# First projections by token tile, loads in a new order, and transposes by DMA in a two-branch attention kernel

## The chip, the cores and the metric

The kernel runs on one core of one Trainium2 chip. The metric is the device time of one execution in microseconds (us), the median of the runs shown. Engines are named as in the profile: PE (TensorE, matmuls), PEld (its weight loads), DVE (VectorE), ACT (ScalarE), POOL (GpSimd), SP (SyncE, which issues most DMAs).

## The reference

```python
def _A_ref(x, wqkv, wo):                       # softmax attention, 32 heads of 16, S = 2048, D = 512
    q, k, v = ...                              # x @ wqkv, split by head
    scores = jnp.einsum("bhqd,bhkd->bhqk", q, k) * (Dh ** -0.5)
    o = jnp.einsum("bhqk,bhkd->bhqd", _softmax(scores), v)
    return o.reshape(B, S, D) @ wo
def _B_ref(x, wqkv, w_phi, wo):                # linear attention with a learned feature map
    pq, pk = einsum("bhsd,hdf->bhsf", q, w_phi), einsum("bhsd,hdf->bhsf", k, w_phi)
    phi = concatenate([softmax(p), softmax(-p)])        # for q and for k
    o = (phi_q @ (phi_k^T v)) / (phi_q @ sum(phi_k) + 1e-6)
    return o.reshape(B, S, D) @ wo
g = _sigmoid((x * gate_w).sum(-1, keepdims=True))
return g * _A_ref(...) + (1 - g) * _B_ref(...)
```

All inputs are bf16; x is 2048 x 512.

## The kernel before

Branch A (softmax attention) carries the time. Its scores are cut into 2048 tiles of 128 keys x 512 queries; four tiles that share keys and queries (four heads) make a pack, 512 packs in all, in the order of query chunk (4 of 512 rows), pair of heads, key tile. For most tiles PE makes the scores in PSUM (`_scores`, L925), ACT takes the exponential of three and then of two tiles in turn (`_exp`, L976), and PE multiplies by V (`_values`, L1045). The score tiles of ACT lie in a ring of five PSUM banks, so the scores of one exponential wait until the exponential before the last has read its banks. 210 tiles go to DVE instead: `SHARES` says how many in each group of 16 packs; `_vector_batch` gathers up to five, copies their scores out of PSUM as integers (`v_bits`, L826) into `vt`, and makes the exponential by a cubic (L848 to L852, L836). `vt` lies over `xn`, the x that was loaded, so its first writes wait until x has been read for the last time.

Branch B is spread between the packs: `_b_fuse` multiplies its q and k weights by the feature map, for which they are transposed (WT, L1146) and multiplied by the block-diagonal `wphi` (L1155); then come keys (`_b_keys`), values and queries, all exponentials on DVE.

At the start x must be transposed, as every projection contracts over its 512 columns. `_x_transpose` does this on PE (L622, four 128x128 blocks per tile of 128 tokens) and DVE or ACT copies them from PSUM to `xT` (L635). For the first 512 tokens, `_proj_q0` and `_proj_k0` project 256 tokens at a time (L682, L651), so that the first packs can start with half the queries; DVE masks q into two sides (L689) and copies k (L665). Weights of branch A lie in `WA` (for q, k and v: a first block of 128 columns, then 384), of branch B in `WB`.

The order of the work on each engine is not written by hand. Every operation is given to a `Plan` with an estimated cost, a latency, its dependences, a priority (`prio`, a due time in packs) and an earliest pack (`rel`); `Plan.order` simulates the engines and writes each engine's list, and the engines then run their lists strictly in order, waiting on semaphores. So a waiting instruction holds up everything behind it on its engine, SP's list of DMAs included. Constants of `_Kernel` (`LEAD`, `QDUE`, `K0`, `SHARES` and so on) steer the plan.

SP's list in the kernel before starts: x tiles 0-1, 2-3, 4-7, the V block of WA, x 8-11, x 12-15, WB for k, eight small DMAs of w_phi into the diagonal blocks of `wphi` (zeroed by POOL before, L542), three blocks of WA, WB for v, WB for q, four transposes into WT (wait for WB for k), four small DMAs of gate_w, eight DMAs that bring the next q into place (L708), WoA, WoB, four transposes into WT (for q). The Q and K blocks of WA are issued by ACT.

Of the kernel before, what the change touches and what calls it, by code (L numbers as in the profile page):

```python
# [10 lines left out]
P = 128  # L11
# [339 lines left out]
class _Kernel:  # L351
# [43 lines left out]
    def _memory(self, ctx):  # L395
# [29 lines left out]
        self.WB = sb("WB", [P, 4, 3 * D], BF16)  # L425
        self.WoA = sb("WoA", [P, 4, D], BF16)
        self.WoB = sb("WoB", [P, 4, D], BF16)
        self.wphi = sb("wphi", [P, 4, P], BF16)
        self.kT = sb("kT", [P, 4, S], BF16)
# [11 lines left out]
        self.WT = sb("WT", [P, 4, D], BF16)  # L441
# [8 lines left out]
        self.onTB = self.WT  # L450
        self.outt = self.WB[:, 0:2, 2 * D:3 * D]
# [21 lines left out]
    def _loads(self):  # L473
# [5 lines left out]
        self.b_WoA, self.b_WoB, self.b_wphi, self.b_gw = B(), B(), B(), B()  # L479
        WA3 = self.A_wqkv.rearrange("(c p) j -> p c j", p=P)  # L480
        x4 = self.x2d.rearrange("(t p) d -> p t d", p=P)

        def load_x(j, halves, lat):
            for h in halves:
                t0, t1 = (4 * j + 2 * h, 4 * j + 2 * h + 2) if len(halves) == 1 else (4 * j, 4 * j + 4)
                if h and len(halves) == 2:
                    continue
                self.dma("SP", f"x{j}{h}", lambda e, t0=t0, t1=t1: e.dma_start(self.xn[:, t0:t1, :], x4[:, t0:t1, :]),
                         writes=[self.b_xn[j][i] for i in halves], prio=-50 + j, lat=lat, cost=0.53)

        def load_wa(s, part, eng, prio, lat):
            lo, hi = (0, P) if part == 0 else (P, D)
            self.dma(eng, f"wa{s}{part}", lambda e: e.dma_start(  # L493
                self.WA[:, s, :, lo:hi], WA3[:, :, D * s + lo:D * s + hi]), writes=[self.b_WA[s][part]], prio=prio,
                lat=lat, cost=0.54 if part == 0 else 1.5)

        load_x(0, [0], 2.8)
        load_x(0, [1], 3.6)
        load_wa(1, 0, "ACT", -50, 3.1)
        load_wa(0, 0, "ACT", -49.9, 3.5)  # L500
        load_x(1, [0, 1], 5.0)
        load_wa(2, 0, "SP", -48.5, 5.4)
        load_x(2, [0, 1], 6.2)
        load_x(3, [0, 1], 7.2)
        load_wa(1, 1, "SP", -46, 7.0)
        load_wa(0, 1, "SP", -45, 6.5)
        load_wa(2, 1, "SP", -44, 6.0)
# [964 lines left out]
```

## Time and profile before

| | |
|---|---|
| runs | 847.53, 847.71, 847.96 us; median 847.71 |
| the profiled execution | 847.48 us, of which the span of the core's work is 845.7 |
| busy in the span | ACT 834.1 us, PE 814.9, DVE 814.6, POOL 7.6 |
| first exponential starts; last one ends | 8.12 us; 840.4 us |
| granted TensorE clock | full (1.00) |

How to read the profile: its chain follows the work that ended last back to the start, with the share of the span of each engine and line. A group's line gives engine, operation, out<-in with shapes and count, then busy time, mean ns of one, and the idle time of the engine just before with what ended it. A timeline line gives start and length in us; instructions of one kind in a row are merged (x12); the bracket is the idle time before. Lines with a "q" behind the engine (SPq) are the issue of DMAs, not their transfer. For DMAs the profile gives the time from issue to landing. In tables by stretch of time, the columns are the stretch, its length, the busy time of each engine, the granted clock, the mean busy share of the 16 DMA engines and GB/s.

### The profile page before, as it was taken

How to read it: one execution, taken by the hardware profiler on the slowest of the kernel's cores; microseconds unless marked ns; L12 is line 12 of the kernel's file. 1: busy time of each engine (PE TensorE's matmuls, PEld its weight loads, DVE VectorE, ACT ScalarE, POOL GpSimd, SP SyncE). 2: the span in 40 equal slices, each digit the busy share in tenths (PEclk: the TensorE clock that was granted, in tenths of full speed). 3: DMA queues.
4: the chain of work that ended last, by engine and by line, in shares of the span. 5: the costliest groups of instructions: out<-in, count | busy, mean ns of one | idle time of the engine just before them, and what ended most of it. 6: DMA issues, size and time to landing. Idle time of an engine off the chain costs nothing.

```text
span 845.7 us, 20062 instructions
## 1 busy us (share of the span) xinstructions
PE 814.9 (96%) x8992; PEld 268.1 (32%) x8992; DVE 814.6 (96%) x1037; ACT 834.1 (99%) x740; POOL 7.6 (1%) x14
## 2 busy tenths in 40 slices
PE   9999999999999999999999999999999999999997
PEld 5324333333322322232323223232322223322244
DVE  5889999999999999999999999999999999999994
ACT  7999999999999999999999999999999999999997
POOL 3000000000000000000000000000000000000000
PEclk9999999999999999999999999999999999999999
DMA  9300000000000000020201102010101102000000
GB/s 261 96 1 8 1 8 1 2 8 5 5 2 7 2 2 8 2 43 3 39 8 33 32 8 44 14 45 13 39 8 27 32 14 39 8 2 1 2 2 27
DMA packets 45222, 19.00 MB, mean 22 GB/s; under 512 B 34897, under 2 KB 45137, under 8 KB 45137
## 3 DMA queue, kind: packets, MB, share of 16 engines
q1 hardware_dynamic: 43936, 17.40, 8.8%
q8 instruction: 70, 1.15, 0.5%
q10 hardware_dynamic: 1200, 0.33, 0.2%
q14 instruction: 16, 0.12, 0.0%
HBM read 6.31 MB, written 2.10 MB: 10 GB/s over the span
## 4 chain that ended last, share of the span: by engine, by line
ACT 97%; SPq 1%; POOL 1%; DMA 0%; PE 0%; DVE 0%; issue 0%; POOLq 0%
ACT ET L976 97%; SPq L1146 1%; DMA WT<-WB 0%; SPq L546 0%; POOL V L535 0%; POOL qT L541 0%; SPq L493 0%; SPq L512 0%; POOL V L537 0%; POOL wphi L542 0%; PE ps L1045 0%; DVE xT L1420 0%; PE ps L1410 0%; PE ps L1155 0%; PE ps L925 0%
## 5 line engine op out<-in xcount | busy, mean ns | idle before, releaser
L976 ACT ACTIVATE ET<-ps 128x1536 bf16<-128x1536 f32 x735 | 831.6, 1389 | 2.1 <-PE ps L925 1.9
L925 PE MATMUL ps<-qT,kT 32*128 32x512 bf16 (+2 forms) x2248 | 317.1, 364 | 24.2 <-ACT ET L976 18.3
L1054 PE MATMUL ps<-kT,zero 128*32 128x512 bf16 (+1 forms) x3272 | 271.0, 384 | 0.0
L1045 PE MATMUL ps<-ET,V 128*32 128x512 bf16 (+2 forms) x2014 | 194.6, 364 | 0.3 <-ACT ET L976 0.3
L925 PEld LDWEIGHTS ps<-qT,kT 32*128 32x128 bf16 x2248 | 83.7, 91 | 311.0 <-ACT ET L976 225.9
L826 DVE TENSOR_SCALAR vt<-ps 128x512 uint32<-128x512 f32 x210 | 137.4, 680 | 2.6 <-PE ps L925 1.9
L836 DVE SCALAR_TENSOR_TENSOR vu<-vt,vu 128x2560 int16<-128x2560 uint32 (+4 forms) x44 | 118.5, 2693 | 0.4
L1054 PEld LDWEIGHTS ps<-kT,zero 128*32 128x32 bf16 x3272 | 72.8, 95 | 116.3 <-issue 89.7
L851 DVE TENSOR_TENSOR vf<-vf 128x2560 f16<-128x2560 f16 (+4 forms) x60 | 81.9, 1365 | 0.5
L848 DVE TENSOR_SCALAR vf<-vt 128x2560 f16<-128x2560 uint8 (+4 forms) x60 | 81.9, 1365 | 0.2
L1045 PE MATMUL ps<-vu,V 128*32 128x512 bf16 (+1 forms) x234 | 76.5, 360 | 0.0
L1045 PEld LDWEIGHTS ps<-ET,V 128*32 128x32 bf16 x2014 | 55.4, 96 | 51.5 <-issue 30.5
L852 DVE TENSOR_TENSOR vu<-vu,vf 128x2560 f16<-128x2560 f16 (+4 forms) x44 | 62.4, 1419 | 0.2
L651 PE MATMUL ps<-WB,xT 128*128 128x512 bf16 x192 | 55.6, 383 | 0.5 <-DVE T L1074 0.2
L1230 DVE TENSOR_TENSOR vt<-bq,bsum 128x2048 uint32<-128x2048 bf16 x16 | 36.5, 2282 | 0.2
L1234 DVE SCALAR_TENSOR_TENSOR bq<-vt,bq 128x2048 int16<-128x2048 uint32 x16 | 36.5, 2280 | 0.1
L651 PE MATMUL ps<-xT,WA 128*128 128x512 bf16 (+1 forms) x128 | 35.5, 376 | 0.0
L850 DVE TENSOR_SCALAR vu<-vf 128x2560 f16<-128x2560 f16 (+4 forms) x44 | 34.5, 785 | 0.3
L1074 DVE STREAM_TRANSPOSE T<-ps 128x512 f32<-128x512 f32 (+1 forms) x35 | 23.1, 659 | 3.5 <-PE ps L1045 3.5
L1045 PEld LDWEIGHTS ps<-vu,V 128*32 128x32 bf16 x234 | 20.9, 96 | 12.6 <-issue 8.5
L1187 DVE TENSOR_SCALAR bq<-ps 128x512 bf16<-128x512 f32 x32 | 21.5, 682 | 1.6 <-PE ps L651 1.6
L651 PEld LDWEIGHTS ps<-WB,xT 128*128 128x128 bf16 x192 | 14.3, 97 | 26.1 <-issue 13.5
(88 smaller groups left out, 407.6 us busy)
## 6 DMA issues: line engine op xcount, KB each, us to landing
qT<-qraw SPq DMA_DIRECT2D x120, 16.0 KB, 1.8
xn<-in_A_x_dram SPq DMA_DIRECT2D x3, 512.0 KB, 6.7
WB<-in_B_wqkv_dram SPq DMA_DIRECT2D x3, 512.0 KB, 8.3
out_dram<-WB SPq DMA_DIRECT2D x12, 128.0 KB, 1.7
WA<-in_A_wqkv_dram SPq DMA_DIRECT2D x3, 384.0 KB, 5.8
xn<-in_A_x_dram SPq DMA_DIRECT2D x2, 256.0 KB, 3.8
WoA<-in_A_wo_dram SPq DMA_DIRECT2D x1, 512.0 KB, 4.1
WoB<-in_B_wo_dram SPq DMA_DIRECT2D x1, 512.0 KB, 5.0
```

The costliest lines, as they stand in the source:

```text
L651: mm = op("PE", lambda e, c=c: e.matmul(self._bank(job)[:, 0:n], lhs(c), rhs(c), start=(c == 0), stop=(c == 3)), self.c_pe(n), reads=reads ...
L826: parts.append(op("DVE", lambda e, j=j, job=job: e.tensor_scalar(vt[:, j, :], self._bank(job), SCALE * LOG2E * 2.0 ** 24, 2.0 ** 31, op0=A ...
L836: o = op("DVE", lambda e: e.scalar_tensor_tensor(out=flat(vu).bitcast(I16), in0=flat(vt), scalar=2.0 ** -17, in1=flat(vu), op0=ALU.mult, o ...
L848: ("_frac", two, lambda e: e.tensor_scalar(vf, frac, 1 / 256, ROOT, op0=ALU.mult, op1=ALU.add), [b_vt], [b_vf]),
L851: ("_sq", two, lambda e: e.tensor_tensor(vf, vf, vf, ALU.mult), [b_vf], [b_vf]),
L852: ("_cube", two, lambda e: e.tensor_tensor(vu, vu, vf, ALU.mult), [b_vf, b_vu], [b_vu]),
L925: ins = e.matmul(out[u][:, cols], self.kT[32 * i:32 * i + 32, cp, kt * TOK:(kt + 1) * TOK], self.qT[32 * i:32 * i + 32, s, q], start=True, ...
L976: o = plan.op("ACT", lambda e: e.activation(self.ET[:, a % NS:a % NS + n, :], self.ps[:, a % NR:a % NR + n, :], ACT.Exp, scale=SCALE), sel ...
L1045: ins = e.matmul(self._bank(ot)[32 * i:32 * i + 32, to], self.V[:, kt, g8 // 2, v0:v0 + 32], tile[:, cols], start=first and j == 0, stop=o ...
L1054: ins = e.matmul(self._bank(ot)[32 * i:32 * i + 32, lo:QCH], self.zero[:], self.kT[:, 0, lo:QCH], start=False, stop=False, tile_position=( ...
L1230: op("DVE", lambda e: e.tensor_tensor(vt.rearrange("p (g f i) -> p g f i", f=DH, i=4), x, top, ALU.subtract), self.c_dve(n), reads=[b, sel ...
L1234: op("DVE", lambda e: e.scalar_tensor_tensor(out=flat.bitcast(I16), in0=vt, scalar=2.0 ** -17, in1=half, op0=ALU.mult, op1=ALU.add), self. ...
```

## The change

- The first two x tiles are projected one by one (`_proj_first`): for each tile four matmuls of 128 columns for Q and four for K, ahead of the transposes of tiles 2 and 3. ACT copies K's first half to `kT`; DVE copies all transposes.
- The K block of WA is issued by SP as its second DMA; only the Q block is issued by ACT. The order of the other loads is new, and x 12-15 and the later blocks get an earliest pack.
- x tiles 8-11 and 12-15 are transposed by one DMA each, from `xn` to `xT`, in place of PE and copies. `xT` is laid out by tile.
- Each transposition into WT is one DMA in place of four. `WB` is laid out by q, k, v.
- w_phi comes by one DMA (`wphin`); POOL multiplies it by a mask of heads into `wphi`. gate_w comes by one DMA.
- The planner's constants and `SHARES` are new; DVE gets 212 score tiles in place of 210.

```diff
-    NB, NVU, LEAD = 5, 3, 16
-    QDUE, VPRIO, VREL, TPRIO = 38.0, -24.0, 161.0, -4.0
+    NB, NVU, LEAD = 5, 3, 1
+    QDUE, VPRIO, VREL, TPRIO = 34, -3.0, 161.0, -4.0
     KEEP = 14
-    EARLY = 23
-    VREL0 = 4
-    FIRST = (1,)
-    LAST = (4, 3)
-    OREL = 1
+    XREL, KD, VD = 4, 6, 5
+    BYDMA = (2, 3)
+    EARLY = 36
+    VREL0 = 1
+    FIRST = (3, 4)
+    LAST = (3, 2)
+    OREL = -4
...
-        self.xT = sb("xT", [P, 4, S], BF16)
+        self.xT = sb("xT", [P, NT, 4, TOK], BF16)
...
+        load_wa(0, 0, "ACT", -50, 3.3)
+        load_x(0, 0, 2, -50, 2.85)
+        load_wa(1, 0, "SP", -49.8, 3.0)
+        load_x(0, 2, 2, -49.5, 3.4)
+        load_x(1, 4, 4, -49, 4.5)
+        load_wb(1, -48.8, 5.5)
+        self.dma("SP", "wphi", lambda e: e.dma_start(self.wphin[:], self.B_w_phi.rearrange("(c a) d f -> (a d) c f", a=8)),
+                 writes=[self.b_wphin], prio=-48.7, lat=5.7, cost=0.53)
+        load_wa(2, 0, "SP", -48.5, 5.7)
+        load_x(2, 8, 4, -48, 6.8)
+        load_x(3, 12, 4, -47, 3.0, self.XREL)
+        load_wa(1, 1, "SP", -46, 4.1, self.XREL)
+        load_wa(0, 1, "SP", -45, 4.6, self.XREL + 1)
+        load_wa(2, 1, "SP", -44, 4.4, self.XREL + 1)
+        load_wb(2, -7, 5.5, 6)
+        self.dma("SP", "gw", ...
+        load_wb(0, -3, 4.5, 8)
...
+        op("POOL", lambda e: e.tensor_tensor(
+            self.wphi[:].rearrange("p c (a f) -> p c a f", a=8), self.wphin[:, :, None, :].to_broadcast([P, 4, 8, 16]),
+            self.heads[:, None, :, None].to_broadcast([P, 4, 8, 16]), ALU.mult), 1.5,
+            reads=[self.b_wphin, self.b_heads], writes=[self.b_wphi], name="wphi_spread", prio=-1)
...
             if j == 0:
-                self._proj_k0(0, 2)
-                self._proj_q0(0, 3)
-                self._proj_q0(1, None)
-                self._proj_k0(1, 4)
+                tiles = self._x_transpose(0, 0, 0)
+                tiles = self._x_transpose(0, 1, 4, self._proj_first(tiles))
+                self._proj_q0(tiles)
+                self._proj_k0(1, None)
             else:
+                if j in self.BYDMA:
+                    self.dma("SP", f"xtr{j}", lambda e, j=j: e.dma_start_transpose(
+                        out=self.xT[:, 4 * j:4 * j + 4].rearrange("p t c q -> p (t c) q"),
+                        in_=self.xn[:, 4 * j:4 * j + 4].rearrange("p t d -> p (t d)")), cost=2.0, reads=self.b_xn[j],
+                        writes=[self.b_xT[j]], prio=-46.4 + 0.9 * (j - 2), lat=2.3)
+                else:
+                    for half in range(2):
+                        self._x_transpose(j, half)
...
+    def _proj_first(self, tiles):
+
+        op = self.plan.op
+        jobs, last = (self._job(3)[0], self._job(2)[0]), []
+        for tt in range(2):
+            for w, job in enumerate(jobs):
+                def run(e, tt=tt, w=w, job=job):
+                    cols = slice(TOK * tt, TOK * tt + TOK)
+                    for c in range(4):
+                        ins = e.matmul(self._bank(job)[:, cols], self.WA[:, w, c, 0:P], self.xT[:, tt, c],
+                                       start=(c == 0), stop=(c == 3))
+                    return ins
+                last.append(op("PE", run, 4 * self.c_pe(128), reads=[self.b_WA[w][0]], deps=[tiles[tt]] + last[-1:],
+                               name="first", prio=-3.0 + 0.1 * tt))
+        self.early[3] = [self._q0_out(0, jobs[0], None, last[2])]
+        o = op("ACT", lambda e: e.activation(self.kT[:, 0, 0:256], self._bank(jobs[1])[:, 0:256], ACT.Copy), 0.35,
+               deps=[last[3]], writes=[self.b_k0[0]], name="kproj_ev", prio=-2.5)
+        self.early[2] = [o]
+        return last
...
-    SHARES = (0, 1, 1, 9, 0, 9, 1, 1, 7, 5, 9, 4, 13, 2, 9, 4,
-              10, 9, 9, 6, 8, 3, 7, 8, 8, 11, 10, 7, 8, 13, 10, 8)
+    SHARES = (1, 2, 3, 5, 3, 3, 2, 10, 2, 6, 6, 1, 14, 4, 4, 10,
+              12, 3, 9, 3, 13, 2, 4, 12, 13, 7, 8, 9, 9, 11, 13, 8)
...
-    K0, SK, Q0, SQ = 11.0, 8.75, 187.0, 14.75
+    K0, SK, Q0, SQ = 6, 9.75, 171.0, 15.5
...
-        self.dma("SP", f"wtr{s}", [lambda e, c=c: e.dma_start_transpose(
-            out=self.WT[:, :, P * c:P * c + P], in_=self.WB[:, c, D * s:D * s + D]) for c in range(4)], cost=5.9,
-            reads=[self.b_WB[s]], writes=[self.b_WT], prio=-6 if s else due, rel=-99 if s else due - 10, lat=2.0)
+        self.dma("SP", f"wtr{s}", lambda e: e.dma_start_transpose(
+            out=self.WT[:].rearrange("p c k q -> p (c k) q"), in_=self.WB[:, s].rearrange("p c j -> p (c j)")), cost=2.0,
+            reads=[self.b_WB[s]], writes=[self.b_WT], prio=-47.5 if s else due, rel=-99 if s else due - 10, lat=2.4)
```

Columns, strides and the names of `xT`, `WB`, `WT` and `onTB` follow the new layouts elsewhere; the shapes of those instructions stay.

More of the change, by code (lines that the diff above doesn't have):

```diff
@@ L624, in tr @@
                 return ins
-            mm = op("PE", tr, 4 * slow * self.c_pe(128), reads=[self.b_xn[j][half], self.b_iden], deps=[mm], name="xtr",
-                    prio=due, rel=min(j, 2) - 1 if j else -99, acquire=pool if apart or t2 == 0 else None)
+            mm = op("PE", tr, 4 * slow * self.c_pe(128), reads=[self.b_xn[j][half], self.b_iden], deps=[mm, *after], name="xtr",
+                    prio=due, rel=1 if j else -99, acquire=pool if apart or t2 == 0 else None)
             if t2 == 0 and bank is None:
```

132 lines of the change are left out of this document (58 added, 74 removed).

## The prediction

> **What bounds the kernel now.** I read the chain that ended last first, then the costliest groups, then the timelines of ScalarE and of SP's queue over the first 40 us, then single DMA landings.
>
> ```profile
> ACT 97%; SPq 1%; POOL 1%; DMA 0%; PE 0%; DVE 0%; issue 0%; POOLq 0%
> ...
> L976 ACT ACTIVATE ET<-ps 128x1536 bf16<-128x1536 f32 x735 | 831.6, 1389 | 2.1 <-PE ps L925 1.9
> ...
> L826 DVE TENSOR_SCALAR vt<-ps 128x512 uint32<-128x512 f32 x210 | 137.4, 680 | 2.6 <-PE ps L925 1.9
> ```
>
> ScalarE's exponentials are the chain: 831.6 us busy, 1.9 us lost to waits. So only three things can move the time: when the first exponential starts, holes in the stream, and how many score tiles ScalarE has (2048 less the 210 of L826). The start:
>
> ```profile
> 4.62 0.76 DVE L635 COPY xT<-ps 128x512 bf16<-128x512 bf16 x2 [2.58 <-PE ps L622]
> ...
> 6.12 0.60 PE L682 MATMUL ps<-xT,WA 128*128 128x256 bf16 x4
> ...
> 6.76 0.48 DVE L689 TENSOR_SCALAR qT<-ps,mask 128x256 bf16<-128x256 f32 x1 [0.47 <-PE ps L682]
> ...
> 7.67 0.39 PE L925 MATMUL ps<-qT,kT 32*128 32x256 bf16 x6
> ...
> 8.12 1.45 ACT L976 ACTIVATE ET<-ps 128x1536 bf16<-128x1536 f32 x1 [1.43 <-PE ps L925]
> ...
> 9.87 13.91 ACT L976 ACTIVATE ET<-ps 128x1024 bf16<-128x1024 f32 x12 [0.30 <-PE ps L925]
> ```
>
> The reader is to see that the first x tiles are transposed and copied by 5.38 (4.62 + 0.76), that Q's projection starts only at 6.12, and that the second exponential waits 0.30. Two more holes of 0.14 and 0.20 stand at 21.28 and 23.79. The exponential of tiles 35-37 (call it G) starts at 24.91, that of tiles 60-62 (H) at 36.27. Then SP's queue:
>
> ```profile
> 12.11 1.06 SPq L512 DMA_DIRECT2D WB<-in_B_wqkv_dram  x2
> 13.21 7.64 SPq L1146 DMA_TRANSPOSE WT<-WB  x4
> ...
> 29.38 0.51 SPq L549 DMA_DIRECT2D WoB<-in_B_wo_dram  x1
> 29.99 5.16 SPq L1146 DMA_TRANSPOSE WT<-WB  x4
> ```
>
> and, asked issue by issue, the time from issue to landing of the second WoB and of the first and last transpose behind it:
>
> ```profile
> WoB<-in_B_wo_dram SPq DMA_DIRECT2D x1, 512.0 KB, 5.0
> ...
> WT<-WB SPq DMA_TRANSPOSE x1, 4.8
> ...
> WT<-WB SPq DMA_TRANSPOSE x1, 2.5
> ```
>
> WoB lands at 29.38 + 5.0 = 34.4; the transpose issued at 29.99 lands at 34.8 and its three successors 0.5 us apart, to 36.35. A transpose thus stands in line behind the loads issued before it on SP. The Trainium skill ("DMA: Bandwidth & Descriptors", "Queues, rings and completion order") says that each DMA engine takes one queue's descriptors in ring order; the trace agrees.
>
> **The change, part by part.** The sum is against this execution: 847.48 us, span 845.7, 1.8 around it; the median of the runs is 847.71.
>
> *First exponential.* The projections of x tiles 0 and 1 no longer stand behind the transposes of tiles 2 and 3. Q's first four matmuls can follow the copy of tile 0, half of the 0.76, at 5.0. Sixteen 128-column matmuls at 56 ns (L622: 16 in 1.06, 8 in 0.62) run from 5.07 to 6.0, plus 0.17 until the last result. DVE's 0.48 from 5.96 and ScalarE's copy of K (0.38, its 256-column row at the end, L1423) from 6.2 end at 6.44 and 6.58; scores at 6.65, and 0.45 later, as now, the exponential: 7.1, **-1.0**. Waiting for the two weight blocks: the first 768 KB land by 5.99 now (4.14, 4.55, 5.39, 5.99), with whichever of them first. The Q block, alone on ScalarE's queue, takes the place of the 4.55; the K block behind 256 KB of x lands by 5.2, when its matmuls are due (5.3). The skill's same page ("Issuing engines are not separate DMA queues") says that a second issuing engine saves only the issue time, so two queues would bring nothing by themselves; I count nothing for them.
>
> *Second exponential.* DVE copies tiles 2 and 3 (6.49 to 7.25), masks (0.42), then Q's second half is ready at 8.17: scores 8.23, exponential 8.65 after the first's end at 8.55. The hole shrinks by **0.2**.
>
> *Transposes by DMA.* PE loses 32 transposes (2 us), DVE four copies of 0.685 (2.7 us); both have idle time here (DVE is busy 17.9 of the first 30 us), so the worth is the two later holes, **-0.3**, if nothing else gates. G would start at 23.5.
>
> *What the DMA queue now carries.* The changed program's SP order is x0, K block, x1, x4-7, WB1, w_phi, V block, x8-11, transpose WT (waits for WB1), transpose x8-11 (waits), x12-15, three 384 KB blocks of WA, WB2, gate_w, transpose x12-15 (waits), WB0, eight q pieces, WoA, WoB, transpose WT again. In before 512 KB takes 1.5 us in line (landings 8.0, 9.5, 11.0, 12.6), 384 KB 1.15, 128 KB 0.53; w_phi is the same 512 pieces of 32 bytes, 9 ns each in the trace, 32 on each of 16 engines: 0.3. So WB1 lands at 9.0, x8-11 at 11.4. A transpose of 512 KB takes 2.0 in line (four at 0.5) and 4.3 from issue on an idle queue (L1297): WT 13.2, x8-11 15.8. x12-15, issued behind it, lands at 17.5; the three blocks need 3.4 more, WB2 1.5, gate_w 0.3, the transpose 2.0: **24.6**, from 17.5.
>
> Who waits for that: in PE's new order the first scores for DVE (vt lies over xn, so they wait until xn has been read) stand directly ahead of eight value matmuls and the scores of G. After the landing come 0.1, 0.45 and 0.4: G starts at 25.6. Against 24.91 that is **+0.7**, and all gains ahead of it are swallowed. The bounds: 23.5 (nothing gates), and +1 us for each time that a transpose waits for a lagging DMA engine. The windows show that this happens:
>
> ```profile
> 13.00:19.00 6.00, 6.00 (x81) 3.46 (x80) 2.67 (x4) 6.00 (x7) 0.00 (x0) 1.00 1.11 327
> 19.00:20.00 1.00, 1.00 (x12) 0.41 (x10) 0.81 (x2) 1.00 (x3) 0.00 (x0) 1.00 2.68 172
> 20.00:21.00 1.00, 1.00 (x11) 0.33 (x7) 0.48 (x1) 1.00 (x1) 0.00 (x0) 1.00 0.33 75
> ```
>
> In the last two columns (busy share, GB/s) the queue falls from 327 to 75 GB/s when the first transpose stands at its head: its packets take up to 1.5 us, until one engine, 1 us late since a 16 KB instruction fetch of 1.02 us at 13.6, has caught up. Such a fetch would now fall into the transposes. I take half of one, **+0.4**.
>
> H gives a second gate: the last WT transpose follows WoB. q can be issued at 22.5 (now 23.0), WoB about 29.3, landing 33.7, the transpose 35.8; its matmuls, four value matmuls and scores add 0.95: 36.75, beside 36.27 now. G at 25.6 or later makes H 36.9 or later, so this costs nothing more; but without the first gate it still takes back what was won.
>
> *w_phi by GpSimd.* Lands at 9.3; the nearest row is gwb's copy of 128x512, 0.91 us. Between 0.9 and 3 (two inputs, one of them float32) it ends by 12.4, before WT (13.2): nothing. It would cost above 4 us.
>
> *212 tiles.* ScalarE has 1836 tiles; pairs of exponentials (5 tiles) start every 2.26 us, so two tiles less give **-0.9**; the last exponential holds one tile in place of three. DVE gets 2 x 2.2 us (0.68 + 7.4/5, rows L826, L836, L848 to L852), loses 2.7, hence +1.9 with the small rest. It is busy 795 of the 810 us between 30 and 840; that it absorbs this is a choice, near the row that shows ScalarE waiting for it nowhere. The tail behind the last exponential keeps its 5.3 us. Layouts of xT, WB and WT change addresses, not shapes: 0, at most 0.1 us per projection, under PE's waits for ScalarE (18.3 us).
>
> **Sum:** 847.48 + 0.7 + 0.4 - 0.9 = 847.7; the early gains are inside the 0.7. Against the median of 847.71 that is no change. 0.2% (1.7 us, about what a measurement of this kernel can tell from no change) puts the borders at 846.0 and 849.4.
>
> **Rivals.**
> 1. *The late transpose doesn't gate* (the queue drains faster, or WT's gate is met too): G 1.4 early and H with it: 847.48 - 1.0 - 0.2 - 0.3 - 0.9 = 845.0. For it: no wait of this kind exists now. Against: the line behind WoB. Chance 0.20. A part of it: if a single 512 KB transpose ran at the loads' rate (1.5 us), the late one would land at 23.0 and H stand at 36.25: 847.48 - 0.9 = 846.6, inside no change; I give this 0.08, out of the forecast's share. The skill's page ("Latency and other measured facts") gives 350 to 400 GB/s for contiguous transposes and 261 otherwise; by it an estimate for 512 KB is 1.3 to 2.0 us. The trace agrees with the slow end (phiT's packets take 2.6 us).
> 2. *Slower: transposes wait for lagging DMA engines.* Two halts of 1.4 us between 11 and 24 us put the x12-15 transpose at 27.4, G at 28.4, +3.5: 850.1. It decides from 2.2 us of halts together (849.4). For: the 1.3 us halt above. Against: one halt among the eight WT transposes of before. Chance 0.12.
> 3. *DVE becomes the bound:* if its 1.9 us find no idle time, the late tiles hold up PE: 847.48 + 0.7 + 1.9 = 850.1. Chance 0.07.
> 4. *It doesn't do what it says:* the first exponential stays near 8.1 as the K block comes late; the queue gates anyway, 847.7. Chance 0.03, inside no change.
>
> Forecast with its own spread (846.0 to 849.4): 0.58, with rival 4 0.61. So faster 0.20, same 0.61, slower 0.19. The range, 844.9 to 850.2, takes in rivals 1 to 3 but for their tails.
>
> **What would show it.** First exponential at 7.1 and second at 8.65; landing of the x12-15 transpose at 24.6; the longest wait of ScalarE about 2 us on PE just before tiles 35-37, and PE's on that DMA; G at 25.6 to 26; H near 37; no further hole. I am wrong if ScalarE runs through 22 to 26 us without a hole, or if holes appear after 40 us.

## The result, and the profile after

The changed kernel takes 853.1 us (median of 6 runs, 851.26 to 856.78) where the kernel before takes 847.62 (6 runs, 847.48 to 847.99): a ratio of 1.0072, 95% interval 1.005 to 1.0094. The forecast was 847.7, no change; the time lies outside its range, on the side of the second rival. The profiled execution of the changed kernel took 855.59, its span 853.7.

The chain, ScalarE's exponentials and VectorE's copies of scores (L860), from the page of the changed kernel:

```profile
ACT 94%; DMA 2%; PE 2%; SPq 1%; DVE 0%; issue 0%
...
L1010 ACT ACTIVATE ET<-ps 128x1536 bf16<-128x1536 f32 x735 | 831.4, 1384 | 10.9 <-PE ps L959 10.8
...
L860 DVE TENSOR_SCALAR vt<-ps 128x512 uint32<-128x512 f32 x212 | 139.8, 683 | 9.4 <-PE ps L959 9.2
```

ScalarE's busy time is the same within 0.2 us (831.4 and 831.6); the idle time before its exponentials has grown from 2.1 to 10.9 us, nearly all of it waits for scores. So the loss is waiting, and ScalarE's timeline says where (start, length, operation, count, idle time before):

```profile
7.36 1.45 ACT L1010 ACTIVATE ET<-ps 128x1536 bf16<-128x1536 f32 x1 [0.87 <-PE ps L959]
9.02 3.28 ACT L1010 ACTIVATE ET<-ps 128x1024 bf16<-128x1024 f32 x3 [0.21 <-PE ps L959]
...
15.70 9.20 ACT L1010 ACTIVATE ET<-ps 128x1536 bf16<-128x1536 f32 x8 [1.14 <-PE ps L959]
30.72 1.45 ACT L1010 ACTIVATE ET<-ps 128x1536 bf16<-128x1536 f32 x1 [5.82 <-PE ps L959]
33.20 1.02 ACT L1010 ACTIVATE ET<-ps 128x1024 bf16<-128x1024 f32 x1 [1.03 <-PE ps L959]
34.71 1.45 ACT L1010 ACTIVATE ET<-ps 128x1536 bf16<-128x1536 f32 x1 [0.48 <-PE ps L959]
37.18 1.02 ACT L1010 ACTIVATE ET<-ps 128x1024 bf16<-128x1024 f32 x1 [1.02 <-PE ps L959]
```

The start is earlier, as forecast (7.36 and 9.02 for 8.12 and 9.87). A hole of 1.14 stands before the exponential of tiles 15-17. G starts at 30.72, 5.8 later than before, and the exponentials after it wait again. What TensorE waits for (its table of waits: us in total, times, longest), and its timeline around G:

```profile
PE ps L959 <- DMA xT<-xn: 4.9, 1, 4.9
...
PE ps L1189 <- DMA WT<-WB: 1.3, 1, 1.3
```

```profile
23.32 0.39 PE L959 MATMUL ps<-qT,kT 32*128 32x512 bf16 x2
28.56 0.60 PE L959 MATMUL ps<-qT,kT 32*128 32x512 bf16 x1 [4.85 <-DMA xT<-xn]
29.09 1.04 PE L1079 MATMUL ps<-ET,V 128*32 128x512 bf16 x8
30.07 0.61 PE L959 MATMUL ps<-qT,kT 32*128 32x512 bf16 x4
```

This is the place that the forecast named: the first score for the vector tiles, waiting for the DMA that transposes x tiles 12-15, with eight value matmuls and G's scores in order behind it. But the wait is 4.85 us, and what comes behind it is slow: one 512-column score takes 0.60 instead of 0.39. SP's queue shows the first reason:

```profile
9.52 2.28 SPq L1180 DMA_TRANSPOSE WT<-WB  x1
11.85 3.52 SPq L585 DMA_TRANSPOSE xT<-xn  x1
15.42 0.58 SPq L493 DMA_DIRECT2D xn<-in_A_x_dram  x1
...
19.90 4.96 SPq L585 DMA_TRANSPOSE xT<-xn  x1
```

The reader is to see the lengths of the issues. The two transposing DMAs of x, behind transfers that are still in the line, keep SP for 3.5 and 5 us: their issues end at 15.37 and 24.86, near the landing of a transfer ahead (WT at 14.9, WB2 at 25.0). So x tiles 12-15 are not asked for before 15.42. The times from issue to landing of WT, of x tiles 8-11 transposed, of the load of x tiles 12-15 and of their transpose are:

```profile
WT<-WB SPq DMA_TRANSPOSE x1, 5.4
xT<-xn SPq DMA_TRANSPOSE x1, 4.8
...
xn<-in_A_x_dram SPq DMA_DIRECT2D x1, 512.0 KB, 4.3
...
xT<-xn SPq DMA_TRANSPOSE x1, 8.6
```

So they land at 14.9, 16.7, 19.7 and 28.5. The table by stretch (stretch, length, busy time and count of PE, PEld, DVE, ACT, POOL, granted clock, DMA share, GB/s) shows two more reasons:

```profile
12.00:13.00 1.00, 1.00 (x9) 0.34 (x6) 0.69 (x1) 1.00 (x2) 0.00 (x0) 1.00 1.28 19
...
27.00:28.00 1.00, 0.00 (x0) 0.00 (x0) 0.00 (x0) 0.00 (x0) 0.00 (x0) 0.88 0.90 70
28.00:29.00 1.00, 0.44 (x1) 0.10 (x1) 0.00 (x0) 0.00 (x0) 0.00 (x0) 0.50 1.09 300
```

At 12 us the DMA engines are busy and move 19 GB/s, at 27 us 70: the packets of the transpose in the line stand still for 1.4 and about 1.0 us, beside 16 KB instruction fetches of 1.04 us (at 11.5) and 0.95 us (at 26.3). And the granted TensorE clock falls to 0.50 at 27.8, 4.1 us after TensorE went idle, and stays there until 38.0. The Trainium skill ("TensorE: Matmul & The Clock Gate", "Part 1: The HAM clock gate") says that the clock is either full or half, that it falls after an idle window of some 3.4 us, and that gaps longer than that are to be avoided. The trace agrees: the fall came 4.1 us into the idle time, and 10.2 us are three such windows.

In shares: 5.8 at G, 3.3 more by H, 0.1 from there to exponential 60, then 1.2 won back by the end (the last exponential holds one tile): 8.0 of span. The other executions fit in the main. The mean granted clock was 0.994 in those of 855.59 and 856.78, 0.996 in 853.27 and 852.92, 0.998 in 852.89 and 851.26; over 853 us that is 10.2, 6.8 and 3.4 us at half clock. Two executions of the same mean clock still differ by up to 1.6 us, so the clock is not the whole spread. The kernel before varies by 0.5.

### The profile page after: what moved, and what is told of

It reads as the page before. It is cut to its first block, busy times and chain, and to the rows that moved or that the text cites. A ratio compares the mean times of both kernels' runs of the same rounds, so it can differ in the third digit from the quotient of the medians.

```text
span 853.7 us, 19855 instructions
## 1 busy us (share of the span) xinstructions
PE 807.6 (95%) x8871; PEld 265.6 (31%) x8916; DVE 818.1 (96%) x1036; ACT 833.7 (98%) x740; POOL 7.9 (1%) x14
## 4 chain that ended last, share of the span: by engine, by line
ACT 94%; DMA 2%; PE 2%; SPq 1%; DVE 0%; issue 0%
ACT ET L1010 94%; DMA xT<-xn 1%; DMA WB<-in_B_wqkv_dram 1%; PE ps L662 1%; PE ps L959 1%; SPq L585 0%; PE ps L1079 0%; SPq L1180 0%; SPq L493 0%; SPq L498 0%; SPq L521 0%; PE ps L1444 0%; PE ps L758 0%; SPq L503 0%; DVE xT L1454 0%
## 5 line engine op out<-in xcount | busy, mean ns | idle before, releaser
L1010 ACT ACTIVATE ET<-ps 128x1536 bf16<-128x1536 f32 x735 | 831.4, 1384 | 10.9 <-PE ps L959 10.8
L1088 PE MATMUL ps<-kT,zero 128*32 128x512 bf16 (+1 forms) x3216 | 264.8, 383 | 0.3 <-issue 0.3
L860 DVE TENSOR_SCALAR vt<-ps 128x512 uint32<-128x512 f32 x212 | 139.8, 683 | 9.4 <-PE ps L959 9.2
L870 DVE SCALAR_TENSOR_TENSOR vu<-vt,vu 128x2560 int16<-128x2560 uint32 (+3 forms) x44 | 119.5, 2717 | 0.2
L1088 PEld LDWEIGHTS ps<-kT,zero 128*32 128x32 bf16 x3216 | 70.5, 94 | 110.4 <-issue 84.9
L885 DVE TENSOR_TENSOR vf<-vf 128x2560 f16<-128x2560 f16 (+3 forms) x60 | 82.5, 1375 | 0.5
L882 DVE TENSOR_SCALAR vf<-vt 128x2560 f16<-128x2560 uint8 (+3 forms) x60 | 82.4, 1374 | 0.2
L886 DVE TENSOR_TENSOR vu<-vu,vf 128x2560 f16<-128x2560 f16 (+3 forms) x44 | 62.8, 1428 | 0.2
L662 PE MATMUL ps<-WB,xT 128*128 128x512 bf16 x164 | 48.9, 388 | 3.8 <-issue 1.6
L884 DVE TENSOR_SCALAR vu<-vf 128x2560 f16<-128x2560 f16 (+3 forms) x44 | 35.0, 795 | 0.2
L1079 PEld LDWEIGHTS ps<-vu,V 128*32 128x32 bf16 x236 | 20.6, 96 | 14.9 <-issue 10.7
```

The source lines that it names most:

```text
L662: mm = op("PE", lambda e, c=c: e.matmul(self._bank(job)[:, 0:n], lhs(c), rhs(c), start=(c == 0), stop=(c == 3)), self.c_pe(n), reads=reads ...
L860: parts.append(op("DVE", lambda e, j=j, job=job: e.tensor_scalar(vt[:, j, :], self._bank(job), SCALE * LOG2E * 2.0 ** 24, 2.0 ** 31, op0=A ...
L870: o = op("DVE", lambda e: e.scalar_tensor_tensor(out=flat(vu).bitcast(I16), in0=flat(vt), scalar=2.0 ** -17, in1=flat(vu), op0=ALU.mult, o ...
L882: ("_frac", two, lambda e: e.tensor_scalar(vf, frac, 1 / 256, ROOT, op0=ALU.mult, op1=ALU.add), [b_vt], [b_vf]),
L885: ("_sq", two, lambda e: e.tensor_tensor(vf, vf, vf, ALU.mult), [b_vf], [b_vf]),
L886: ("_cube", two, lambda e: e.tensor_tensor(vu, vu, vf, ALU.mult), [b_vf, b_vu], [b_vu]),
```

## The experiments

The theory after the result: the loss is the place of a few DMAs in SP's list, above all that of the transpose of x tiles 12-15, and the halved clock that follows TensorE's wait. Rivals: that the clock is the loss; that the lists of the new plan cost the time wherever the DMAs stand; that the gains (earlier start, two tiles fewer) are not there.

All runs in one table. The middle columns are the shift of an exponential of the profiled execution against the same one before (index 5, 13, G, H, 60; us); "before" is the kernel before, run beside each.

| run | 5 | 13 | G | H | 60 | span | median (runs) | before | ratio, 95% interval |
|---|---|---|---|---|---|---|---|---|---|
| changed kernel | -0.9 | -0.1 | +5.8 | +9.1 | +9.2 | 853.7 | 853.10 (6) | 847.62 | 1.0072 (1.0050 to 1.0094) |
| e1_fill | -1.2 | -0.2 | +4.6 | +4.9 | +5.0 | 850.3 | 852.21 (4) | 847.61 | 1.0054 (1.0037 to 1.0070) |
| e2_line | -0.8 | -0.5 | -0.5 | +2.7 | +2.7 | 851.6 | 852.30 (5) | 847.61 | 1.0046 (1.0027 to 1.0065) |
| e3_pe_x | -0.5 | +4.1 | +4.1 | +8.4 | +8.5 | 855.6 | 857.55 (4) | 847.61 | 1.0119 (1.0104 to 1.0134) |
| e4_pe_x12 | -1.0 | -0.2 | -0.2 | +13.1 | +14.5 | 861.9 | 862.13 (4) | 847.61 | 1.0172 (1.0157 to 1.0187) |
| e5_sp_a | -0.8 | +0.9 | +0.9 | +4.1 | +5.1 | 849.7 | 852.02 (4) | 847.40 | 1.0056 (1.0040 to 1.0073) |
| e6_sp_b | -0.9 | +4.1 | +4.1 | +5.9 | +6.0 | 850.5 | 852.28 (4) | 847.40 | 1.0059 (1.0044 to 1.0074) |
| e7_sp_c | -0.8 | +1.7 | +1.6 | +1.6 | +1.8 | 846.3 | 848.21 (10) | 847.51 | 1.0006 (0.9996 to 1.0016) |
| e8_sp_d | -0.3 | +2.5 | +2.4 | +2.4 | +2.4 | 846.9 | 847.91 (10) | 847.51 | 1.0005 (0.9996 to 1.0015) |
| e9_c_fill | -0.5 | +0.4 | +0.4 | +0.9 | +1.0 | 845.5 | 848.03 (11) | 847.46 | 1.0006 (0.9998 to 1.0015) |
| e10_sp_e | -0.8 | +1.7 | +2.6 | +3.5 | +3.6 | 848.1 | 849.90 (5) | 847.46 | 1.0035 (1.0021 to 1.0048) |
| e11_e_fill | -0.7 | +1.9 | +2.8 | +4.2 | +4.4 | 848.9 | 850.06 (5) | 847.46 | 1.0034 (1.0022 to 1.0047) |
| e12_c_pe | -0.8 | -0.3 | +0.4 | +1.2 | +1.3 | 845.8 | 847.80 (11) | 847.37 | 1.0006 (0.9997 to 1.0015) |
| e13_f | -1.0 | 0.0 | -0.1 | -0.1 | +0.1 | 844.6 | 846.80 (11) | 847.36 | 0.9993 (0.9984 to 1.0002) |
| e14_f2 | -1.0 | -1.3 | -1.3 | +0.6 | +0.7 | 845.2 | 847.32 (11) | 847.25 | 1.0002 (0.9993 to 1.0011) |
| e15_f3 | -1.0 | -1.4 | -1.4 | +0.8 | +0.9 | 845.4 | 847.71 (11) | 847.47 | 1.0005 (0.9996 to 1.0014) |

The profiled execution is one of those counted and not always near the median: those of the changed kernel (855.59), e4 (863.80) and e8 (849.16) are among the longest of theirs.

### The clock alone (e1)

```diff
-            return self._scores(e, units, {...})
+            ins = self._scores(e, units, {...})
+            for _ in range(20 if units[0] == 33 else 0):
+                self._fill(e, self.ot[0])          # four matmuls that add zeros
+            return ins
```

> The changed kernel with 80 matmuls that add zero (20 x 4, full array, 0.21 us each set) behind the scores of tiles 33-34, so that PE is busy while it would wait for the transpose of x tiles 12-15. Theory (the wait of 4.9 us is one cost, the halved PE clock from 27.8 to 38 us a second one that the idle time brings): the granted clock stays at 1.00, tiles 35-37 start their exponential at about 29.6 as before the halving 1.0 us behind the landing, no holes follow, and the time falls by about 3 us, to 850 to 851. Rival (the clock falls for another reason, such as the load or the moment): clock 0.50 again, 853.

TensorE's timeline of this run around G, and ScalarE's G:

```profile
23.55 4.50 PE L1091 MATMUL ps<-kT,zero 128*32 128x512 bf16 x80
28.24 0.39 PE L959 MATMUL ps<-qT,kT 32*128 32x512 bf16 x1 [0.20 <-DMA xT<-xn]
...
29.54 10.64 ACT L1013 ACTIVATE ET<-ps 128x1536 bf16<-128x1536 f32 x9 [4.73 <-PE ps L959]
```

The 80 matmuls fill the wait, the score behind it takes 0.39 again, the clock stays full in all four runs, and from G to H the shift grows by 0.3 instead of 3.3. G itself is still 4.6 late. All four runs lie within 0.11 us, where those of the changed kernel lie within 5.5: most of that spread goes with the clock. So the halved clock is a consequence of the idle time. It is worth 3.4 us between the two profiled executions (spans 853.7 and 850.3), but only 0.9 between the medians (853.10 and 852.21), as most executions of the changed kernel spend less time at half clock than the profiled one. The expected 850 to 851 was missed for this reason. The rest of the loss, 4.6 of 5.5 by the medians, is there with the clock at full.

### The planner told of the line, and x transposed by TensorE (e2, e3, e4)

```diff
 # e2: Plan.order, when an SP operation is placed (SERVICE: 0.3 to 1.6 us by size, TURN = 2.8)
+                    turn = o.name.startswith(("dma_wtr", "dma_xtr"))
+                    service = self.TURN if turn else self.SERVICE[o.name]
+                    if turn:
+                        o.end = free[e] = max(o.end, self.line)
+                    self.line = max(self.line, o.start + (2.1 if turn else 2.6)) + service
+                    o.lat = self.line - o.end
 # e3: e2, and    BYDMA = ()      all x tiles by TensorE, and vt's first half waits for x tiles 0-11 only
 # e4: the changed kernel with    BYDMA = (2,)      only x tiles 8-11 by DMA
```

> The changed kernel, same work and same instructions, but the planner is told that SP's DMAs are served one behind the other: each lands no earlier than the one before plus its own service (1.5 us for 512 KB, 1.2 for 384 KB, 2.8 for a transpose). Only the order of the lists changes; no PE instruction that waits for the transpose of x tiles 12-15 stands early any more. Theory (the loss is PE's list standing behind a DMA that comes late): no wait over 1 us after 16 us, full clock, exponential of tiles 35-37 at 24 to 24.5, time 846 to 847. Rival (212 tiles make DVE the bound): the early hole goes, but holes come after 40 us, 849 to 851. Rival (transposes by DMA as such, halted by late engines): holes of 1 to 3 us stay before 40 us, 848 to 850.

> As e2, and all x tiles transposed by PE and DVE again (no DMA transposes of x; the two of WT stay), and the first bits of vt wait only for the x tiles that they overwrite. Theory: as in e2 no long wait; PE and DVE carry 2 to 3 us more in the first 30 us, so the exponentials may have holes of up to 1 us before 25 us: 846 to 847.5. If it is clearly faster than e2, the DMA transposes of x cost more than they save.

> The changed kernel with only x tiles 12-15 transposed by PE again, the planner unchanged (it does not know of the line on SP's queue). Theory: the wait for the transpose of x tiles 12-15 is gone, but the planner now puts the transpose of WT for q ahead of the q pieces and its matmuls before the 18th exponential, where by the line (WB for q lands at about 27, the transpose 4 us later) PE waits again, 3 to 5 us: 849 to 853, with the wait on WT from 27 to 31 us. Rival (only the x transposes cost): 846 to 847.

In all three the wait at G is gone (-0.5 and -0.2 there in e2 and e4), and none comes near the kernel before. A new plan writes all lists anew, and each brought a wait of its own: 3.28 us before exponential 16 in e2 (value matmuls queued behind the projection of keys 12-15), 5.05 and 4.36 before exponentials 12 and 18 in e3 without any wait for a DMA (transposes and eight projections ahead of the scores), 13.21 before exponential 18 in e4, which begins with 2.33 on the second WT and goes on with projections at half the clock (from 32.1 to 38.9). Another 4.1 us of e2 are lost near 449 and 657 us, behind falls of the clock far from any DMA wait; its one execution at full clock took 849.21. ScalarE's timeline of e4:

```profile
42.60 3.71 ACT L1010 ACTIVATE ET<-ps 128x1536 bf16<-128x1536 f32 x3 [13.21 <-PE ps L959]
```

All three missed their expected times; e4's wait on WT came where it was expected, but the hole was 13 us and not 3 to 5. Such runs change too much at once to price one DMA. The runs that follow leave the lists of VectorE, ScalarE and GpSimd as the changed kernel has them, and reorder a few entries of SP's, later of TensorE's.

### SP's list alone (e5 to e8)

```diff
 # names in SP's list; the changed kernel has
 #      x8-11, WT, xT 8-11, x12-15, wa11, wa01, wa21, WB2, gate_w, xT 12-15, WB0, q, WoA, WoB, WT(q)
+# e5:  x8-11, WT, x12-15, xT 8-11, wa01, xT 12-15, wa21, wa11, WB2, gate_w, WB0, q, WoA, WoB, WT(q)
+# e6:  x8-11, x12-15, WT, xT 8-11, xT 12-15, wa01, wa21, wa11, WB2, gate_w, WB0, q, WoA, WoB, WT(q)
+# e7:  x8-11, WT, xT 8-11, x12-15, wa01, xT 12-15, wa21, wa11, WB2, gate_w, WB0, q, WT(q), WoA, WoB
+# e8:  as e7, but  WB0, WT(q), q, WoA, WoB
```

(xT is the transpose of those x tiles, wa01, wa11 and wa21 are the 384-column blocks for q, k and v, WT(q) the second transpose into WT.)

> Only SP's list of the changed kernel is written anew (the lists of TensorE, VectorE, ScalarE and GpSimd stay the same, instruction for instruction): x tiles 12-15 are loaded behind the transpose of the linear weights instead of behind the transpose of x tiles 8-11, and their transpose stands ahead of two of the three big weight blocks, of WB2 and of gate_w. Theory (the loss is the place of that transpose in SP's line and what follows from it): it is issued near 16 and lands at 20 to 22 us instead of 28.5, before G's instruction needs it at 23.7; TensorE's wait of 4.9 goes, the clock stays at 1.00, G starts within 0.3 us of the kernel before's 24.91, the shift stays so, and the end is a tile earlier: 846.7 us (845.9 to 847.7). Rival 1 (the wait is only the first of several: WB2, the two blocks or the second WT become the next to be late): a hole of 2 us or more between 25 and 50 us, 849 to 853. Rival 2 (the lists of the 212-tile division cost the time themselves, wherever the DMAs stand): holes without a DMA wait, as in the run with the planner's model of the line, 850 or more.

> As the run before it, but x tiles 12-15 are loaded ahead of the transpose of the linear weights and their transpose stands right behind that of tiles 8-11, ahead of all three big weight blocks. Theory: the load is ahead of the transposing DMAs in the ring, so WT lands about 1.3 us later (16.2 instead of 14.9) and the hole before the exponential of tiles 15-17 grows from 1.1 to about 2.4; both transposes of x are through by 20; block wa01 lands at 22 to 23 and meets its matmul at exponential 12 (about 23) nearly in time. G is up to 1 us later than in the kernel before, the end 847.5 us (846.3 to 849). Rival (the order within the line hardly matters so long as all is through before 24): as the run before it, within 0.4 us of it.

In e5 x12-15 are transposed at 22.7 instead of 28.5 and TensorE doesn't wait for them. The hole of 5.8 is gone, and the first rival came true: the second WT, behind WoA and WoB in the line, lands at 38.7 and costs 3.3 at H. In e6 the first WT is later too (16.6 for 14.9), and the clock halves from 15.6 to 22.4. Both missed their expected times; e6 is level with e5, as its rival said, but loses the time in other places.

> Only SP's list again, the other four engines' as in the changed kernel. x tiles 12-15 stay behind the transpose of tiles 8-11, as in the change, so that nothing of exponentials 6 to 9 is later than there; their transpose goes ahead of two big weight blocks, WB2 and gate_w, as in e5; and the second WT goes behind the eight q pieces but ahead of WoA and WoB, which held it in e5 to 38.6 us. Theory (each wait so far was a place in SP's line, and the transposes of x12-15 and of the second WT are the two that count): x12-15 transposed by 22, G within 0.3 us of 24.91; the second WT lands at 33.5 to 35 and its matmul, wanted near 34, waits less than 1; no clock loss; the end one tile earlier: 846.9 us (846.2 to 848.0). Rival 1 (a third wait comes up behind these two): a further hole of over 1.5 us before 60 us, 848.5 to 851. Rival 2 (the loss is not in the first 50 us): no holes there and still over 849.

> As e7, with the second WT ahead of the eight q pieces too, right behind WB0. Theory: SP stands for WB0 until about 27.5, the second WT lands at 30 to 31, four us before its matmul; the q pieces land near 35, 13 us before their scores (near 48); so no hole at H even if the halts by instruction fetches hit again: 846.6 us (846.0 to 847.4), and not over e7. Rival 1: the q pieces, or WoA and WoB behind them, become late instead: a hole between 44 and 60 us, 848 to 851. Rival 2 as in e7.

With both moved, 4.8 and 5.1 of the 5.5 us that the change had cost are back: 0.7 and 0.4 are left, inside what the interval can tell from no change. No instruction of the four computing engines was touched. That is the theory's test: the places of a few DMAs in SP's list, above all of the two transposes, are the loss. (The blocks of WA, WB2 and gate_w, which the transpose of x tiles 12-15 passes, change places too.) What ScalarE waits for TensorE's scores, in us, times and longest, in the changed kernel, e7 and e8:

```profile
ACT ET L1010 <- PE ps L959: 10.8, 8, 5.8
...
ACT ET L1010 <- PE ps L959: 3.1, 4, 1.3
...
ACT ET L1010 <- PE ps L959: 3.4, 4, 1.7
```

Neither run reached its expected time; both stay about 2 late behind the wait on the first WT. The table by stretch of e7 shows why:

```profile
13.00:14.00 1.00, 0.76 (x7) 0.32 (x6) 0.69 (x1) 1.00 (x2) 0.00 (x0) 1.00 0.50 107
14.00:15.00 1.00, 0.00 (x0) 0.00 (x0) 0.00 (x0) 0.65 (x1) 0.00 (x0) 1.00 1.28 287
15.00:16.00 1.00, 0.78 (x10) 0.46 (x11) 0.35 (x1) 0.01 (x1) 0.00 (x0) 1.00 1.27 289
16.00:17.00 1.00, 1.00 (x13) 1.00 (x12) 0.96 (x2) 1.00 (x1) 0.00 (x0) 0.53 0.52 111
17.00:18.00 1.00, 1.00 (x8) 0.46 (x6) 0.41 (x2) 0.44 (x1) 0.00 (x0) 0.50 0.43 129
```

TensorE idles for 1.46 us in one piece, is busy for 1.5 of 3, and the clock halves for 3.4 us; ScalarE then waits twice more (0.77, 0.45). Not every execution does this: in five of e7's ten the mean granted clock is 1.000 (median span 846.0, that of the others 846.3), and in five of e8's ten (845.0 and 846.6).

### The wait on the first WT (e9 to e12)

```diff
 # e9: e7, and ahead of the first matmul on WT, in the bank that it takes
+            for _ in range(6):
+                e.matmul(bank, self.kT[:, 0, 0:P], self.kT[:, 0, 0:QCH], start=True, stop=True)
 # SP's list: e7   x0-1, K, x2-3, x4-7, WB1, w_phi, V, x8-11, WT, ...
+#            e10  x0-1, K, x2-3, WB1, x4-7, w_phi, V, WT, x8-11, ...
 # e11: e10, and e9's matmuls, four of them
 # e12: e7, and in TensorE's list the scores of exponentials 6 and 7 ahead of the first group on WT, of 8 ahead of the third
```

> e7 with six 512-column matmuls on TensorE (1.3 us at the full clock, results overwritten at once) ahead of the first matmul on WT, in the bank that it takes anyway, so that TensorE works through most of its wait of 1.5 us there; nothing else differs. Theory (what e7 still loses is the halved clock from 16.1 to 19.5 us that follows that wait, 2.5 us of shift between exponentials 5 and 13): the clock stays at 1.00, the hole before exponential 6 stays at 1.1 to 1.5, those before 7 and 8 go, the shift at 13 falls from +1.7 to about +0.3 or below, and the time to 846.9 us (846.3 to 847.5), with less spread than e7's 847.3 to 848.6. Rival (the wait itself and the transposes' lateness make the holes at 7 and 8, the clock only goes with them): the shift at 13 stays over +1.2, 848 us.

> e7 with the loads at the head of SP's list in another order: WB1 ahead of x tiles 4-7, and its transpose ahead of the load of x tiles 8-11, so that WT comes through before them. Theory (the wait at exponential 6 is WT's place in the line): WB1 lands at 8.1 instead of 9.7, WT at 12.2 to 13.7, so its matmul (13.7) waits under 0.3; x tiles 4-7 land at 9.6, where TensorE takes them at 9.4 (0.2 to 0.4 later); x tiles 8-11 transposed by 16.5; no halved clock; shift at 13 below 0, one tile less at the end: 846.4 us (845.8 to 847.1). Rival (the first eight microseconds are as tight as the rest: x tiles 4-7 later than 9.6 stop TensorE, and the wait only changes its name): a hole of 1 us or more before exponential 3, 4 or 5, 847.5 or more.

> e10 with four of e9's matmuls (0.85 us) ahead of the first matmul on WT. Theory: where e10 has no wait left there, the four cost 0.3 to 0.9 us on TensorE beside the exponentials and nothing at the end: within 0.3 us of e10; where a halt still leaves a wait of 1 us, they keep the clock, and this is up to 1.5 us below e10. Rival (TensorE is tight there): the four push scores and projections back, 0.5 to 1 us over e10.

> e7 with TensorE's list changed at three places: the scores of exponentials 6 and 7 stand ahead of the first of the four groups of matmuls on WT (which wait for it), those of exponential 8 ahead of the third; VectorE, ScalarE, GpSimd and SP as in e7. Theory (the hole of 1.5 us before exponential 6 is nothing but the scores standing in order behind an instruction that waits for WT until 15.2): the wait on WT stays at about 1 us, but the holes before exponentials 6 to 8 go (under 0.3 each); the shift at 13 is between -0.9 and 0 if the clock stays at 1.00, the end one tile earlier: 846.2 us (845.6 to 847.0), which is under the kernel before. Rival 1 (the wait, now about 1 us of idle TensorE, still halves the clock as in e7): no hole before 6 but 1 to 2 us before 8 to 10, 847.5 to 848.5. Rival 2 (VectorE's list, where the casts of WT's matmuls stand ahead of V's and the keys', is what holds): a hole of 1 us or more before exponential 9 to 13 with TensorE waiting for VectorE, 847.5 or more.

e9 keeps the clock at full and the two following holes go: the shift at 13 falls from 1.7 to 0.4, as expected. The median hardly follows (848.03 for 848.21), as half of e7's executions had the full clock without the filling. The median span is 845.8, that of the kernel before 845.6; between span and time there lie 1.8 to 3.3 us, where the kernel before has 1.8 to 1.9; what that is stays open. In e10 the wait only changes its name, as its rival said, though it stands at a later exponential than the rival named: WT comes in time (the hole before 6 is 0.3), the transpose of x8-11 lands at 19.6 and costs 2.6 before exponential 9; e11 has nothing left to fill and is level with it. e12 shows that the hole before exponential 6 is nothing but order on TensorE: with two scores ahead of the waiting group it is gone, the shift at 6 is -0.8. Then 1.0, 0.7 and 0.7 are lost before 9, G and H. None beats the kernel before.

### Are the gains there? (e13 to e15)

```diff
 # SP's list: e5's head, e7's end (WT(q) ahead of WoA and WoB). TensorE's list, against e12's:
+# e13: keys 8-11 (which wait for xT 8-11) behind the scores of exponential 10; scores of 11 right behind them
+# e14: also scores of 10 ahead of the first value matmuls; value matmuls of packs 2, 3 and scores of 12 ahead
+#      of the value projection of tiles 8-11; scores of 13 and 14 and value matmuls of pack 4 ahead of the query projection
+# e15: also scores of 15 ahead of the first score for the vector tiles, of 16 ahead of keys 12-15, of 17 behind
```

> The orders of e5 and e7 together on SP (x tiles 12-15 loaded behind the first WT, so that both transposes of x stand early; the second WT ahead of WoA and WoB), and on TensorE e12's order with one thing more: the projection of keys 8-11, which waits for its transpose, goes behind the scores of exponential 10 instead of ahead of those of 9, and the scores of 11 right behind it. VectorE, ScalarE and GpSimd as in the changed kernel. Theory (what e9 and e12 still lose of the forecast gains is three short waits of 0.6 to 0.9 us, before exponentials 9, 14 and 24; the earlier start and the two tiles fewer are worth 0.8 and 1.5): x12-15 transposed at 22.7, the second WT at 33 to 34, no hole over 0.3 before exponential 60, shift at exponential 60 between -0.9 and -0.3, 846.0 us (845.4 to 846.8), under the kernel before by 0.1 to 0.25%. Rival (the gains are not there: without these waits ScalarE stands in others of the same length, behind VectorE or between TensorE's projections): a shift of 0.5 or more at exponential 60 and 847.2 to 848.2, as e9 and e12.

> e13 with the rest of TensorE's list between exponentials 10 and 14 in the order in which ScalarE asks for it: the scores of 10 ahead of the first value matmuls, the value matmuls of packs 2 and 3 and the scores of 12 ahead of the value projection of tiles 8-11, the scores of 13 and 14 ahead of the query projection that follows; nothing is left out, and all other lists are e13's. Theory (e13's two holes of 0.6 before exponential 10 and 0.9 before 12 are TensorE's order alone, and the gains of the change are there): the shift stays between -1.0 and -0.5 through exponential 60, the holes before 10 and 12 are under 0.4 each; the tail gains 1.5: 845.9 us (845.3 to 846.6), ratio 0.997 to 0.999. Rival (VectorE's casts between 15.6 and 22.4 are what ends those waits, so that the holes only move): a shift of -0.3 to +0.3 at exponential 60, 846.8 us as in e13.

> e14 with TensorE's list put in ScalarE's order three scores further: those of exponential 15 ahead of the first score for the vector tiles (which needs the transpose of x12-15), those of 16 ahead of the projection of keys 12-15, those of 17 right behind it. All other lists as before. Theory (e14's one hole of 1.9 before exponential 15 is again only TensorE's order, and the gains of 0.9 at the start and 1.5 at the end are there): no hole over 0.4 before exponential 60, a shift of -1.4 to -0.7 there, 845.6 us (845.0 to 846.4), ratio 0.997 to 0.999, an interval under 1. Rival (TensorE has no slack between 19 and 28 us, so whatever is put back comes up as the next wait): a hole of 1 us or more between exponentials 17 and 26, 846.8 to 847.4 us as in e13 and e14.

e13 has no wait for a DMA over 0.3 us and is the lowest of all: 846.80 beside 847.36, ratio 0.9993 with an interval (0.9984 to 1.0002) that holds no change. Its span is 844.6 (median of the runs; 845.5 before). It loses 0.6 and 0.9 before exponentials 10 and 12. e14 takes these away and keeps a shift of -1.3 up to G, then loses 1.9 before exponential 15; e15 takes that away and loses 2.2 in pieces of at most 0.9 behind it. e13 lies at the upper edge of its expected range, e14 and e15 above theirs. Its table by stretch:

```profile
20.00:22.00 2.00, 2.00 (x29) 1.11 (x27) 0.69 (x1) 1.95 (x3) 0.00 (x0) 1.00 1.25 285
22.00:24.00 2.00, 2.00 (x16) 0.60 (x13) 0.69 (x1) 2.00 (x3) 0.00 (x0) 1.00 0.98 252
24.00:26.00 2.00, 2.00 (x20) 0.52 (x19) 1.73 (x3) 1.88 (x2) 0.00 (x0) 1.00 1.07 361
26.00:28.00 2.00, 2.00 (x13) 0.59 (x10) 0.97 (x3) 1.52 (x2) 0.07 (x1) 1.00 0.94 268
28.00:30.00 2.00, 2.00 (x13) 0.71 (x11) 1.97 (x4) 1.18 (x2) 0.54 (x1) 1.00 0.36 104
```

TensorE is busy throughout these ten microseconds while ScalarE falls from 2.00 to 1.18. This fits e15's rival, though no single hole reaches the 1 us that it named: with the DMA waits gone, TensorE has no slack there, and an order that serves one exponential earlier takes it from a later one. That is argued from waits that only move; no run takes work off TensorE, and in the kernel before TensorE is busy for 9.5 of the same ten microseconds while ScalarE is busy for 9.65. So the gain at the start is real (0.3 to 1.2 us at exponential 5 in every run), but none keeps it past H. The gain at the end is kept by the changed kernel and by every run from e5 on: the span is 1.2 less than the shift at exponential 60 says (changed kernel 9.2 and 8.0, e13 0.1 and -1.1, e15 0.9 and -0.3). The new plans of e2 to e4 lose time behind exponential 60 instead (e4 14.5 and 16.2).

## Why the prediction was wrong

The mechanism was right: the late transpose of x tiles 12-15, TensorE standing in order at the first score for the vector tiles, the early gain swallowed there, halts beside instruction fetches, and the second WT as the next gate (e5 showed it). What failed are the sizes of this gate and one missing term.

1. *First and second exponential:* forecast 7.1 and 8.65, measured 7.36 and 9.02. Worth 0.85 instead of 1.2.
2. *"What the DMA queue now carries", the step that failed:* landings forecast at 13.2 (WT), 15.8, 17.5 (x12-15) and 24.6, measured 14.9, 16.7, 19.7 and 28.5. The line was worked out as if SP's issues took no time. In fact the second transpose's issue held SP from 11.85 to 15.37, so x12-15 were asked for only at 15.42 and landed 2.2 late: 0.9 because the transpose ahead was late, the other 1.3 with the late issue. And there were two halts, 1.4 and about 1.0 us, where +0.4 was taken. G's shift is +5.8 against +0.7 and +0.4. (The terms listed for the late transpose add up to 24.7 and those of the first rival to 845.1, each 0.1 off the recorded figure, which decides nothing.) The kernel before had shown a long issue: of the 7.64 us in the prediction's line for four quarter-size transposes, the first took 3.63, as its chain in order of time has it (start, length):

```profile
13.21 3.63 SPq L1146
```

3. *Landing to G:* 1.0 forecast, 2.2 measured, and another 3.3 by H. The step counted TensorE's work behind the wait at the full clock. The price of 4.85 us of idle TensorE, half the clock for 10.2 us, is in no term and no rival. e1, at full clock, has 1.3 from landing to G and 0.3 more by H; the clock is worth 3.4 us of span between the profiled executions and 0.9 between the medians.
4. *A hole before tiles 15-17:* none forecast. WT came at 14.9 for 13.2, and four matmuls on it stand ahead of scores (1.14; with the clock 2.4 in e7).
5. *The second rival* (850.1) had the halts and the place; "it decides from 2.2 us of halts together" was met by the 2.4 found. It was too cheap by the issue times and by the clock, and its 0.12 was too little: the 75 GB/s that the prediction showed at the head of a transpose is a halt, and the change puts three into the line ahead of G.
6. *H's second gate* 36.75 forecast: in the changed kernel hidden behind G's, as said. Freed in e5, the second WT landed at 38.7 instead of 35.8, and cost 3.3.
7. *w_phi on GpSimd, layouts, VectorE:* nothing, as forecast (the spread takes 1.06 us from 9.85 and ends before WT). VectorE's list is not what bounds, as e7 and e8 leave it as it is and lose only 0.4 to 0.7; the third rival fell.
8. *212 tiles:* -0.9 forecast, -1.2 found: the last exponential is 1.1 shorter, the tail behind it 0.4 shorter (4.9 for 5.3), and 0.3 is lost on the way.

## What to carry to other kernels

Before a load is moved behind a transposing DMA, count the issue as well as the transfer: in these traces a 512 KB transpose behind transfers in the line kept its issuer for up to 5 us, and everything behind it in the list started that much later. Price a wait of TensorE by its length and by the clock that may follow; after a wait of 1.5 us the clock fell in e7's profiled execution, and cheap matmuls in the wait kept it at full in e1 and e9. And when an early gain is forecast, look at how full the next engine is over the following ten exponentials: in these runs an earlier start of 0.3 to 1.2 us was never kept past H.

## What the runs showed of the hardware

- The clock can halve after less than a full idle window. In e7 it fell at 16.1 us, after 1.46 us without a matmul (1.5 us busy of 3), for 3.4 us. In e2 it fell at 444.9, after pauses of 0.68 and 0.30 us close together (1.56 us busy of 2), for 6.8 us, and at 653.1, after a pause of 0.95, for 3.4 us, both far from any DMA wait. A wait of 1.26 us in the changed kernel (before 14.93) and one of 2.65 us in e10 (before 19.60) left it at full. What decides is not shown. The Trainium skill's page ("TensorE: Matmul & The Clock Gate", "Part 1: The HAM clock gate") names idle windows of about 3.4 us that run freely; the length of the half-clock stretches (3.4, 6.8, 10.2) agrees, the threshold does not.
- Issues of 512 KB transposing DMAs took 1.8 us with nothing ahead (e7, at 32.17) and up to 4.96 behind other transfers (the changed kernel, at 19.90). Most plain loads took 0.45 to 0.6, two in the changed kernel 1.85 and 1.55 (at 4.52 and 18.30). What sets the length is not shown: in the kernel before, quarter-size transposes behind WoA and WoB took 1.2 to 1.3 each.
- In e2 to e4, whose lists are all planned anew, the median lies from 0.8 us under to 9 us over the changed kernel's, where no part of the change was forecast to be worth more than 1.1.
